# Three shared buffers for parts and fifth product, a tile of group 0 in another PSUM bank, and one relu part placed earlier

## The chip, the cores and the metric

The program runs on one core of one Trainium2 chip. The metric is the time of one execution on the device, in microseconds (us). The kernel before the change was run three times: 630.22, 631.93 and 632.46 us, median 631.93. The profiled execution, from which all rows here are read, took 632.26 us itself; its span from the first to the last instruction is 630.5 us, so 1.76 us lie around the span.

## The reference, cut to what matters

Three layers follow each other on 1152 tokens of width 512: windowed attention (8 heads), a soft mixture of four experts, and a dense layer with a rational activation.

```python
attn = softmax(where(mask, scale * q @ k.T, -1e9)) @ v        # 2 x 8 heads x 576 x 64
x = attn.transpose(0, 2, 1, 3).reshape(1152, 512)
p = domain_probs / (domain_probs.sum(-1, keepdims=True) + 1e-9)
x = sum(p[:, e:e+1] * (relu(x @ w1[e]) @ w2[e]) for e in range(4))   # hidden width 1024
h = x @ w_in                                                   # 2048 wide; w_in, w_out in float64
g = (a0 + a1*h + a2*h**2 + a3*h**3) / (1 + |b0|*|h| + |b1|*h**2 + 1e-6)
out = g @ w_out
```

## The kernel before, in words

Tokens lie in three chunks `c` of 384 (nine token tiles `t` of 128, three in each chunk). The hidden widths of both matrix layers are cut into units `u` of 256 columns. Units 0 to 15 belong to the experts, units 16 to 23 to the dense layer; two units make a group `g` (groups 0 to 7 experts, 8 to 11 dense). For a unit and a chunk a *first product* (`h_bank`, line 467) makes the hidden values in PSUM (tile `ps_h`), and for a group and a token tile a *second product* (`o_half`, line 513, once for each of the group's two units) makes 128 x 512 outputs in PSUM (tile `ps_o`). Operands are kept as a high part and a low part, so a product is three passes: high by high, high by low, low by high. In most units two of the three chunks are made together in seven smaller products instead (`product`, lines 943 and 1246); the fifth of them is copied to SBUF (`p5`) and added to other products in PSUM by VectorE (lines 969 and 1263).

PSUM has eight banks: two for `ps_o`, four for the two-bank tiles `ps_h` of the pool `psh`, two for a third `ps_h` tile (pool `psh3`, used by every third `h_tile()` that is not told otherwise). During attention the last two hold `ps_s`.

What sets the order of work:

- *Attention* follows the table `ATTENTION`.
- *The experts* (`for g in range(NG1)`) are written in the order of TensorE. Work for VectorE and ScalarE is put between by a planner: `Pace.pe` is TensorE's planned time, `Pace.dv` VectorE's. `later(wait, cost, key, f)` gives a step a due time of `Pace.pe + wait`; when TensorE's planned time passes it, the step is written. Gaps are filled (`fill`) with prepared steps (weight splits at lines 829 and 833, token sums) and with the conversion of the dense weights from float64 words (`convert`, lines 241 to 311), which is needed only by the dense part. So one changed wait shifts VectorE's planned time, and with it the order of all later filling on VectorE, ScalarE and SP. `settle(key)` writes a pending step at once when TensorE needs it.
- *The dense part* follows the table `DENSE`. In it `o9.6.0` is the second product of group 9, token tile 6, first unit; `z9.6` moves that tile out of PSUM; `P5.22` is the fifth product of unit 22, `F22` its copy to SBUF, `v22` and `q22` the two adds that read it. For groups 9 and 10 `z` is a copy by ScalarE into a buffer `part` (line 1162) and a DMA by GpSimd's queue that adds the buffer to `acc[t]` in SBUF (line 1163). There are 18 such tiles and 6 fifth products. The next use of a buffer waits until its DMA has landed, or, for `p5`, until `q` has read it.

The pools that the change touches: `part` had two buffers and `p5` one of its own in pool `late` (lines 1161 and 1259).

Of the kernel before, what the change touches and what calls it, by code (L numbers as in the profile page):

```python
# [18 lines left out]
F32 = mybir.dt.float32  # L19
# [10 lines left out]
NT, DM = 1152, 512  # L30
# [4 lines left out]
TC = 384  # L35
# [60 lines left out]
COST = dict(h=2.09, p=1.045, o=2.74, osum=0.78, relu=1.0, add=0.59, split=0.68, sums=0.42, bits=0.41, both=1.15, token=1.0)  # L96
# [5 lines left out]
def body(ctx, tc, qkv, mask, dp, w1, w2, w1d, w2d, coef, out):  # L102
# [15 lines left out]
    def h_tile(last=None):  # L118

        count[0] += 1  # L120
        last = third and count[0] % 3 == 0 if last is None else last
        pool = third[0] if last else psh
        return pool.tile([128, 2, 512], F32, tag="h", name="ps_h")
# [337 lines left out]
    def h_bank(u, c, i, ps, ks=range(4)):  # L461
        wh, wl = weight(w1s, u, 4)
        xh, xl = xt[c]
        for k in ks:
            f = slice(i * 128, (i + 1) * 128)
            for n, (a, b) in enumerate(((wh, xh), (wh, xl), (wl, xh))):
                nc.tensor.matmul(  # L467
                    ps[:, i, :TC], lhsT=a[:, k, f], rhs=b[:, k],
                    start=k + n == 0, stop=k + n == 5,
                )  # L470
# [46 lines left out]
    def o_bank():  # L517
        return pso.tile([128, 512], F32, tag="o", name="ps_o")
# [11 lines left out]
    def by_dma(g, t):  # L530
        return (1, 3) <= (g, t) < (NG1 - 1, 0)
# [28 lines left out]
    class Rational:  # L560
# [53 lines left out]
        def high(self):  # L614
            self.hh, self.hl = new_h(self.u, self.c)
            nc.scalar.copy(self.hh, self.u1)
# [6 lines left out]
    with tc.manual_schedule():  # L623
# [83 lines left out]
        def small_loads():  # L707
# [5 lines left out]
            v=lambda r: units[r].load_values(),  # L713
# [3 lines left out]
            g=small_loads,  # L717
# [78 lines left out]
        def later(wait, cost, key, f):  # L796
            Pace.due.append((Pace.pe + wait, cost, key, f))
# [102 lines left out]
        def h_begin(u, c, last=None):  # L900
            settle(("w1", u))
            begun[u, c] = h_tile(last)
            h_bank(u, c, 0, begun[u, c])
            passed(COST["h"])

        def h_paced(u, c, last=None):
            if (u, c) not in begun:
                h_begin(u, c, last)
            ps = begun[u, c]
            h_bank(u, c, 1, ps)  # L910
            passed(COST["h"])
            high, low = relu_parts(u, c, ps)
            high()
            later(1.1, COST["relu"], ("h", u, c), low)

        def o_paced(g, t, wait=0.0):
            for v in range(2):
                settle(("h", 2 * g + v, t // 3))
                settle(("w2", 2 * g + v))
            ps = o_bank()  # L920
            for v in range(2):
                o_half(g, t, v, ps)
            passed(COST["o"])
            if by_dma(g, t):
                if wait:
                    later(wait, 0.0, ("o", g, t), lambda: o_sum(g, t, ps))
                else:
                    o_sum(g, t, ps)
            else:
                later(0.2, COST["osum"], ("o", g, t), lambda: o_sum(g, t, ps))  # L930
# [100 lines left out]
        for g in range(NG1):  # L1031
            u = 2 * g
            again = g + 1 in BLOCKED
            o = lambda *at: [(o_paced, *i) for i in at]
            if g == 0:
                later(0.0, COST["osum"], ("o", 0, 3), lambda: o_sum(0, 3, ps_2[3]))
                token_sums()
                tokens_later(temp[0], *(t[:, 0] for t in tt))
                sums_later(2)
                sums_split_later(2, 1)  # L1040
                o_paced(0, 4)
                o_paced(0, 5)
                for v in range(2):
                    h_paced(v, 2)
                tokens_later(temp[2], *(t[:, :2] for t in xt[2]), "first")
                sums_split_later(2, 0)
                tokens_later(temp[1], *(t[:, 1] for t in tt), "second")
                sums_later(3)
                tokens_later(temp[3], *(t[:, 2] for t in tt), "third", begin_conversion)
                continue  # L1050
            a, b = (Blocks(v) for v in (u, u + 1))
            w2_loads = (load_w2, u + 2), (load_w2, u + 3)
            free = [(load_w1, u + 3)] * (g > 1) + [w2_loads[0]] * (g == 1) + [w2_loads[1]]
            free = [(weights_free, *free)] if again else []
            run = lambda g, *ts: [o_paced(g, t, 1.5 * (n == 2)) for n, t in enumerate(ts)]

            def next_sums():
                if again:
                    sums_later(u + 2)
                    sums_split_later(u + 2, 1)  # L1060
                    split_later(w2s, "w2", u + 2)
                    split_later(w1s, "w1", u + 3)
                else:
                    loads((load_w1, u + 3))

            if g == 1:
                sums_split_later(u + 1, 1)
                split_later(w1s, "w1", u + 2)
                a.first(False)
                o_paced(0, 6)  # L1070
                a.sixth()
                a.fifth()
                a.sum_up(0.8, False)
                o_paced(0, 7)
                a.seventh()
                a.second()
                sums_split_later(u + 1, 0, free)
                o_paced(0, 8)
            else:
                for v in (u, u + 1):  # L1080
                    new_h(v, 0)
                h_paced(u, 0, False)
                sums_split_later(u + 1, 1)
                split_later(w2s, "w2", u + 1)
                if again:
                    split_later(w1s, "w1", u + 2)
                run(g - 1, 6, 7, 8)
                a.first(False)
                h_paced(u + 1, 0, True)
                a.fifth()  # L1090
                a.sixth()
                a.sum_up(0.2, False)
                run(g - 1, 3, 4)
                sums_split_later(u + 1, 0, free)
                o_paced(g - 1, 5, 1.5)
                a.seventh()
                a.second()
            b.first(True)
            a.third()
            a.fourth()  # L1100
            next_sums()
            b.fifth()
            b.sixth()
            b.sum_up(0.2, False)
            run(g, *range(3 if again else 1))
            b.seventh()
            b.second()
            if again:
                h_begin(u + 2, 0, False)
            else:  # L1110
                o_paced(g, 1)
            b.third()
            b.fourth()
            if g == 1:
                Window.spare[:] = [None, lone[:, 0], lone[:, 1]]
            if again:
                sums_split_later(u + 2, 0, [(loads, (load_w1, u + 4))])
                sums_later(u + 3)
            else:
                loads(*w2_loads, (load_w1, u + 4), (load_w1, u + 5))  # L1120
# [11 lines left out]
        early_open, late = tc.tile_pool(name="early", bufs=1), []  # L1132
# [3 lines left out]
        ps_h, ps_2, p5_ps, p5s, x2_ps, turned, copied, rational = {}, {}, {}, {}, {}, set(), {}, {}  # L1136
# [18 lines left out]
        def sum_up(g, t, cols=0):  # L1155
            ps, s = ps_2.pop((g, t, cols)), columns(cols)
            if g == NG1:
                acc[t] = accp.tile([128, DM], F32, tag=f"acc{t}", name=f"acc{t}")
                nc.scalar.copy(acc[t], ps)
            elif NG1 < g < NG - 1:  # L1160
                part = late[0].tile([128, DM], F32, tag="part", name="part", bufs=2)
                nc.scalar.copy(part, ps)  # L1162
                nc.gpsimd.dma_start(acc[t], part, accum_op=ALU.add)  # L1163
            elif cols:
                nc.vector.tensor_tensor(out=acc[t][:, s], in0=ps, in1=acc[t][:, s], op=ALU.add)
                store(t, s)
            else:
                o_sum(g, t, ps)
# [86 lines left out]
        def fifth(u):  # L1255
            if not late:
                early_open.__exit__(None, None, None)
                late.append(ctx.enter_context(tc.tile_pool(name="late", bufs=1)))
            p5s[u] = late[0].tile([128, TC], F32, tag="p5", name="p5")
            nc.scalar.copy(p5s[u], p5_ps[u])  # L1260

        def add_fifth(i, u):
# [4 lines left out]
        def of(name):  # L1267
# [3 lines left out]
            h=bank, o=second, O=lambda *a: second(*a, of="h"), z=sum_up, x=turn, X=x_high, Y=x_low, W=x_whole,  # L1271
            T=token_sum, C=sum_high, S=sum_low, P=product, Z=seed, F=fifth,
            v=lambda u: add_fifth(0, u), q=lambda u: add_fifth(1, u),
# [116 lines left out]
```

## Time and profile before

| | |
|---|---|
| median of three runs | 631.93 us |
| profiled execution | 632.26 us, span 630.5 us |
| TensorE matmul busy | 621.4 us, 99% of the span |
| VectorE busy | 522.0 us, 83% |
| ScalarE busy | 371.9 us, 59% |
| GpSimd busy | 88.4 us, 14% |
| mean granted TensorE clock | 0.997 |

The table is read by its first busy row: TensorE works nearly the whole span, so a change of the time has to come from its few idle stretches, from its clock, or from new idle stretches. The experts' part runs from about 80 to 410 us, the dense part from there to the end. In stretches of 5 to 20 us the granted clock is 1.00 everywhere but from 560 to 570 us and at the very end.

### The profile page before, as it was taken

How to read it: one execution, taken by the hardware profiler on the slowest of the kernel's cores; microseconds unless marked ns; L12 is line 12 of the kernel's file. 1: busy time of each engine (PE TensorE's matmuls, PEld its weight loads, DVE VectorE, ACT ScalarE, POOL GpSimd, SP SyncE). 2: the span in 40 equal slices, each digit the busy share in tenths (PEclk: the TensorE clock that was granted, in tenths of full speed). 3: DMA queues.
4: the chain of work that ended last, by engine and by line, in shares of the span. 5: the costliest groups of instructions: out<-in, count | busy, mean ns of one | idle time of the engine just before them, and what ended most of it. 6: DMA issues, size and time to landing. Idle time of an engine off the chain costs nothing.

```text
span 630.5 us, 9862 instructions
## 1 busy us (share of the span) xinstructions
PE 621.4 (99%) x3728; PEld 556.0 (88%) x3728; DVE 522.0 (83%) x788; ACT 371.9 (59%) x682; POOL 88.4 (14%) x103
## 2 busy tenths in 40 slices
PE   8999999999999999999999999999999999989997
PEld 4888898999999999999999999898989989969886
DVE  7687488798888888888888898839999998979894
ACT  6787625364555555555555555346786887768660
POOL 2223330011111111111111111000000011120110
PEclk9999999999999999999999999999999999989999
DMA  9944302368789679788778789762221484471233
GB/s 295 318 141 166 115 8 68 100 181 247 209 227 247 208 218 249 214 221 237 220 223 234 227 263 247 252 269 105 97 100 43 150 275 101 105 206 25 50 84 116
DMA packets 39535, 111.28 MB, mean 177 GB/s; under 512 B 4256, under 2 KB 5024, under 8 KB 37440
## 3 DMA queue, kind: packets, MB, share of 16 engines
q1 hardware_dynamic: 29104, 92.14, 43.4%
q0 software_dynamic: 9936, 18.09, 16.4%
q8 instruction: 29, 0.48, 0.3%
q10 hardware_dynamic: 448, 0.43, 0.3%
q14 instruction: 18, 0.15, 0.1%
HBM read 67.13 MB, written 25.43 MB: 147 GB/s over the span
## 4 chain that ended last, share of the span: by engine, by line
PE 70%; issue 25%; DMA 1%; DVE 1%; POOL 1%; ACT 0%; POOLq 0%; ACTq 0%
PE ps_o L513 33%; PE ps_h L467 14%; PE ps_h L943 12%; PE ps_o L943 2%; PE ps_h L1246 2%; PE ps_v L431 2%; DMA acc<-part 1%; PE ps_s L417 1%; PE ps_h L513 1%; POOL acc L1163 1%; PE ps_s L362 1%; PE ps_h L655 1%; PE ps_o L1246 0%; DVE mx L390 0%; DVE pr L380 0%
## 5 line engine op out<-in xcount | busy, mean ns | idle before, releaser
L513 PE MATMUL ps_o<-w,hh 128*128 128x512 f32 x848 | 229.1, 392 | 2.8 <-ACT part L1162 2.6
L513 PEld LDWEIGHTS ps_o<-w,hh 128*128 128x128 f32 x848 | 157.8, 188 | 34.3 <-ACT part L1162 3.0
L513 PE MATMUL ps_o<-w,hl 128*128 128x512 f32 x424 | 131.1, 391 | 0.1
L467 PE MATMUL ps_h<-xh,w 128*128 128x384 f32 x464 | 126.0, 338 | 0.0
L513 PEld LDWEIGHTS ps_o<-w,hl 128*128 128x128 f32 x424 | 79.6, 188 | 17.5 <-DVE hl L489 0.6
L467 PEld LDWEIGHTS ps_h<-xh,w 128*128 128x128 f32 x464 | 84.4, 188 | 1.2 <-issue 0.3
L544 POOL DMA_DIRECT2D acc<-part x51 | 45.3, 889 | 258.0 <-ACT part L543 201.1
L467 PE MATMUL ps_h<-xl,w 128*128 128x384 f32 x232 | 77.6, 334 | 0.0
L543 ACT ACTIVATE part<-ps_o,p_sb 128x512 f32<-128x512 f32 x51 | 35.1, 688 | 48.8 <-issue 22.7
L485 ACT ACTIVATE hh<-ps_h 128x768 fp32r<-128x768 f32 x48 | 39.0, 812 | 42.1 <-PE ps_h L943 31.6
L489 DVE SCALAR_TENSOR_TENSOR hl<-ps_h,hh 128x768 fp32r<-128x768 f32 x48 | 45.0, 951 | 4.0 <-ACT hh L485 3.7
L1163 POOL DMA_DIRECT2D acc<-part x18 | 15.6, 868 | 204.1 <-ACT part L1162 197.9
L467 PEld LDWEIGHTS ps_h<-xl,w 128*128 128x128 f32 x232 | 43.6, 188 | 0.1
L969 DVE TENSOR_TENSOR ps_h<-ps_h,p 128x384 f32<-128x384 f32 x28 | 15.8, 566 | 23.3 <-PE ps_h L943 23.3
L271 ACT ACTIVATE x<-x 128x512 f32<-128x512 f32 x32 | 21.7, 677 | 22.7 <-DVE t L268 20.5
L943 PE MATMUL ps_h<-t,sw 128*128 128x384 f32 x168 | 34.0, 337 | 0.0
L396 ACT ACTIVATE pr<-pr,mx 128x80 f32<-128x80 f32 (+1 forms) x84 | 29.7, 358 | 6.0 <-DVE mx L390 4.7
L833 DVE TENSOR_TENSOR w<-raw,w 128x512 fp32r<-128x512 f32 x48 | 32.8, 684 | 0.5 <-ACT w L829 0.5
L943 PEld LDWEIGHTS ps_h<-t,sw 128*128 128x128 f32 x168 | 29.9, 188 | 1.2
L943 PE MATMUL ps_h<-xh,w 128*128 128x384 f32 x104 | 29.7, 335 | 0.0
L573 ACT ACTIVATE ab<-ps_h,absb 128x768 f32<-128x768 f32 x24 | 21.8, 907 | 13.3 <-DMA w<-w 7.9
L592 DVE TENSOR_TENSOR u<-ps_h,u 128x768 f32<-128x768 f32 x24 | 22.9, 953 | 7.6 <-ACT u L577 6.1
(162 smaller groups left out, 1145.8 us busy)
## 6 DMA issues: line engine op xcount, KB each, us to landing
acc<-part POOLq DMA_DIRECT2D x69, 256.0 KB, 5.5
raw<-in_w_dram SPq DMA_DIRECT2D x32, 512.0 KB, 6.4
w<-w SPq DMA_DIRECT2D x14, 1024.0 KB, 6.3
w<-lone SPq DMA_DIRECT2D x18, 512.0 KB, 4.6
x<-in_w1d_dram SPq DMA_DIRECT2D x16, 512.0 KB, 4.5
x<-in_w2d_dram SPq DMA_DIRECT2D x16, 512.0 KB, 5.5
w<-w SPq DMA_DIRECT2D x14, 512.0 KB, 5.9
sw<-sw SPq DMA_DIRECT2D x12, 512.0 KB, 5.8
```

Source lines behind the costliest of these rows:

```text
L396: nc.scalar.activation(pr[:, j, i], pr[:, j, i], AF.Exp, scale=-1.0, bias=self.mx[:, j, i:i + 1], accum_out=self.total[:, j, i:i + 1],)
L467: nc.tensor.matmul(ps[:, i, :TC], lhsT=a[:, k, f], rhs=b[:, k], start=k + n == 0, stop=k + n == 5,)
L485: nc.scalar.activation(hh, ps[:, :, :TC], AF.Relu)
L489: nc.vector.scalar_tensor_tensor(out=hl, in0=ps[:, :, :TC], scalar=0.0, in1=hh.bitcast(F32), op0=ALU.max, op1=ALU.subtract,)
L513: nc.tensor.matmul(ps, lhsT=a[:, i, tk], rhs=b[:, i, cols], start=v + n == 0, stop=v + n == 6)
L543: nc.scalar.activation(part, ps, AF.Copy, scale=pe)
L544: nc.gpsimd.dma_start(acc[t], part, accum_op=ALU.add)
L573: nc.scalar.activation(self.ab, self.ps, AF.Abs, scale=absb[:, 0:1])
L592: nc.vector.tensor_tensor(out=self.u1, in0=self.ps, in1=self.u1, op=ALU.mult)
L833: nc.vector.tensor_tensor(out=w[:, 1, s_], in0=raws[nm, u][:, s_], in1=w[:, 0, s_].bitcast(F32), op=ALU.subtract)
L943: nc.tensor.matmul(out, lhsT=a[i][:, k], rhs=b[j][:, k], start=first and k + n == 0, stop=k + n == 3, skip_group_check=not first,)
L1163: nc.gpsimd.dma_start(acc[t], part, accum_op=ALU.add)
```

## The change

Three edits.

1. The buffers of `part` in the dense part become three, and `p5` is taken from the same three (`tag="part"`, the first 384 of 512 columns) instead of having one buffer of its own. A buffer is handed out in the order in which buffers come free.
2. The tile of `o_paced(0, 4)` (group 0, token tile 4) is put into the first bank of an `h_tile()` instead of an `o_bank()`. This `h_tile()` is the one that falls on the third pool; the tiles of units 0 and 1, chunk 2, come one place later in the rotation and both lie in `psh`.
3. For unit 1, chunk 2, the low part of relu (line 489, `hl`) is due 0.1 us after its planned time instead of 1.1.

```diff
-        def h_paced(u, c, last=None):
+        def h_paced(u, c, last=None, wait=1.1):
...
-            later(1.1, COST["relu"], ("h", u, c), low)
+            later(wait, COST["relu"], ("h", u, c), low)
-        def o_paced(g, t, wait=0.0):
+        def o_paced(g, t, wait=0.0, ps=None):
...
-            ps = o_bank()
+            ps = ps if ps is not None else o_bank()
...
-                o_paced(0, 4)
+                o_paced(0, 4, ps=h_tile()[:, 0])
                 o_paced(0, 5)
                 for v in range(2):
-                    h_paced(v, 2)
+                    h_paced(v, 2, wait=1.1 - v)
...
-                part = late[0].tile([128, DM], F32, tag="part", name="part", bufs=2)
+                part = late[0].tile([128, DM], F32, tag="part", name="part", bufs=3)
...
-            p5s[u] = late[0].tile([128, TC], F32, tag="p5", name="p5")
+            p5s[u] = late[0].tile([128, DM], F32, tag="part", name="p5", bufs=3)[:, :TC]
```

TensorE's order is the same before and after but for the name of the bank of `o_paced(0, 4)`. GpSimd's is the same too. ScalarE's order in the dense part is the same; what changes there is what the copies wait for. The first place is ScalarE from `z9.8` to `z10.1`; `DMASW` with a digit is the semaphore of an adding DMA (they go round eight, so that `z9.6` to `z10.1` signal 1, 2, 3, 4, 5), `PE_49`, `DVE_49` and `Activation_49` are those of the engines. Before:

```order
L1162 COPY part<-ps_o 128x512 [waits DMASW1_49,PE_49,Activation_49]
L586 ACTIVATE ab<-sq,cbias 128x768 [waits DVE_49,Activation_49]
L577 ACTIVATE u_5549<-ps_h,na 128x768 [waits Activation_49]
L573 ACTIVATE ab<-ps_h,absb 128x768
L589 ACTIVATE ab<-ab 128x768 [waits Activation_49]
L1162 COPY part<-ps_o 128x512 [waits DMASW2_49,PE_49]
L586 ACTIVATE ab<-sq,cbias 128x768 [waits DVE_49]
L577 ACTIVATE u_5574<-ps_h,na 128x768 [waits DVE_49]
L1162 COPY part<-ps_o 128x512 [waits DMASW3_49,PE_49]
```

After the change, the same nine:

```order
L1162 COPY part<-ps_o 128x512 [waits PE_49]
L586 ACTIVATE ab<-sq,cbias 128x768 [waits DVE_49,Activation_49]
L577 ACTIVATE u_5549<-ps_h,na 128x768 [waits Activation_49]
L573 ACTIVATE ab<-ps_h,absb 128x768
L589 ACTIVATE ab<-ab 128x768 [waits Activation_49]
L1162 COPY part<-ps_o 128x512 [waits DMASW1_49,PE_49]
L586 ACTIVATE ab<-sq,cbias 128x768 [waits DVE_49]
L577 ACTIVATE u_5574<-ps_h,na 128x768 [waits DVE_49]
L1162 COPY part<-ps_o 128x512 [waits DMASW2_49,PE_49]
```

Nothing moved; `z9.8` waits for no DMA any more, `z10.0` for the one of `z9.6` instead of `z9.7`, `z10.1` for the one of `z9.7` instead of `z9.8`.

The second place is VectorE at the two relu parts of chunk 2 in group 0 (`hl_1278` of unit 0, `hl_1311` of unit 1; `xl2` the low part of a token sum; `sw` the low part of summed weights). Before:

```order
L489 SCALAR_TENSOR_TENSOR hl_1278<-ps_h_1242,hh_1277 128x768
L862 TENSOR_TENSOR sw_1294<-raw_767,sw_1294 128x512
L893 TENSOR_TENSOR xl2_122<-ab_1203,xh2_121 128x768
L489 SCALAR_TENSOR_TENSOR hl_1311<-ps_h_1280,hh_1310 128x768
L862 TENSOR_TENSOR sw_1322<-raw_767,sw_1322 128x512
```

After:

```order
L489 SCALAR_TENSOR_TENSOR hl_1278<-ps_h_1242,hh_1277 128x768
L862 TENSOR_TENSOR sw_1294<-raw_767,sw_1294 128x512
L489 SCALAR_TENSOR_TENSOR hl_1311<-ps_h_1280,hh_1310 128x768
L893 TENSOR_TENSOR xl2_122<-ab_1203,xh2_121 128x768
L862 TENSOR_TENSOR sw_1337<-raw_767,sw_1337 128x512
```

Unit 1's relu part went ahead of `xl2`.

The third place is VectorE just ahead of the tenth add of a fifth product (line 969), as one of many places where the filling of the experts' part shifted. Before:

```order
L311 SCALAR_TENSOR_TENSOR sums<-x_2194,sums 128x512
L258 TENSOR_SCALAR t<-x_2270 128x512
L862 TENSOR_TENSOR sw<-raw,sw 128x512
L268 SCALAR_TENSOR_TENSOR t<-x_2270,t 128x512
L969 TENSOR_TENSOR ps_h<-ps_h,p_2227 128x384
```

After:

```order
L311 SCALAR_TENSOR_TENSOR sums<-x_2172,sums 128x512
L258 TENSOR_SCALAR t<-x_2254 128x512
L268 SCALAR_TENSOR_TENSOR t<-x_2254,t 128x512
L245 TENSOR_TENSOR w<-sums,w 128x512
L862 TENSOR_TENSOR sw<-raw,sw 128x512
L167 TENSOR_TENSOR sums<-sums 128x2x128 x3
L969 TENSOR_TENSOR ps_h<-ps_h,p_2228 128x384
```

More of the conversion (lines 245 and 167) now stands ahead of this add.

## Rows read from the trace of the kernel before

**Rows 1.** The page's first part: busy time, share, instructions of each engine.

```profile
PE 621.4 (99%) x3728; PEld 556.0 (88%) x3728; DVE 522.0 (83%) x788; ACT 371.9 (59%) x682; POOL 88.4 (14%) x103
```

**Rows 2.** Waits of TensorE: engine, line waited for, total us, times, longest.

```profile
PE ps_o L513 <- ACT part L1162: 2.6, 1, 2.6
...
PE ps_o L513 <- DVE xl L455: 0.3, 1, 0.3
```

**Rows 3.** Stretches: length, busy PE, PEld, DVE, ACT, POOL, granted clock, DMA share, GB/s.

```profile
560.00:565.00 5.00, 2.50 (x6) 2.02 (x7) 1.72 (x2) 2.89 (x4) 0.88 (x1) 0.74 0.82 214
565.00:570.00 5.00, 5.00 (x27) 4.90 (x27) 4.96 (x7) 2.52 (x4) 0.87 (x1) 0.92 0.44 76
```

**Rows 4.** Timeline of TensorE, 553 to 575: start, length, instruction, idle before.

```profile
558.41 1.07 PE L513 MATMUL ps_o<-w,hh 128*128 128x512 f32 x4
559.32 0.61 PE L513 MATMUL ps_o<-w,hl 128*128 128x512 f32 x2
562.50 2.07 PE L513 MATMUL ps_o<-w,hh 128*128 128x512 f32 x4 [2.56 <-ACT part L1162]
...
570.71 0.33 PE L1246 MATMUL ps_o<-xh,sw 128*128 128x384 f32 x1
```

**Rows 5.** Timeline of ScalarE around the same wait.

```profile
557.66 0.88 ACT L589 ACTIVATE ab<-ab 128x768 f32<-128x768 f32 x1
561.86 0.59 ACT L1162 COPY part<-ps_o 128x512 f32<-128x512 f32 x1 [3.32 <-DMA acc<-part]
...
563.18 0.98 ACT L577 ACTIVATE u<-ps_h,na 128x768 f32<-128x768 f32 x1
564.22 0.59 ACT L1162 COPY part<-ps_o 128x512 f32<-128x512 f32 x1
```

**Rows 6.** Line 1163, the adding DMA: two single ones, then all eighteen.

```profile
L1163 POOL DMA_DIRECT2D acc<-part x1: 872/872/872, 548.2 to 548.2; - x1
DMA to landing us min/median/max: 5.8/5.8/5.8
...
L1163 POOL DMA_DIRECT2D acc<-part x1: 859/859/859, 552.8 to 552.8; - x1
DMA to landing us min/median/max: 9.0/9.0/9.0
...
DMA to landing us min/median/max: 3.2/3.3/9.1
```

**Rows 7.** Timeline of TensorE, 74 to 102: group 0's second products.

```profile
77.04 0.61 PE L513 MATMUL ps_o<-w,hl 128*128 128x512 f32 x2
77.93 1.19 PE L513 MATMUL ps_o<-w,hh 128*128 128x512 f32 x4 [0.28 <-DVE xl L455]
...
94.30 1.08 PE L513 MATMUL ps_o<-w,hh 128*128 128x512 f32 x4
95.51 0.73 PE L513 MATMUL ps_o<-w,hl 128*128 128x512 f32 x2
96.08 1.21 PE L943 MATMUL ps_h<-t,sw 128*128 128x384 f32 x6
```

**Rows 8.** Timeline of ScalarE, 74 to 104: relu of unit 1, chunk 2.

```profile
92.06 0.81 ACT L485 ACTIVATE hh<-ps_h 128x768 fp32r<-128x768 f32 x1 [1.87 <-PE ps_h L467]
```

**Rows 9.** Timeline of VectorE at five places of the argument.

```profile
93.63 0.96 DVE L893 TENSOR_TENSOR xl<-ab,xh 128x768 fp32r<-128x768 f32 x1 [2.33 <-ACT xh L890]
94.50 0.95 DVE L489 SCALAR_TENSOR_TENSOR hl<-ps_h,hh 128x768 fp32r<-128x768 f32 x1
...
201.13 0.57 DVE L969 TENSOR_TENSOR ps_h<-ps_h,p 128x384 f32<-128x384 f32 x1 [1.45 <-PE ps_h L943]
...
564.19 0.96 DVE L592 TENSOR_TENSOR u<-ps_h,u 128x768 f32<-128x768 f32 x1 [3.28 <-ACT u L577]
...
573.06 0.57 DVE L1263 TENSOR_TENSOR ps_h<-ps_h,p 128x384 f32<-128x384 f32 x1 [1.34 <-PE ps_h L1246]
```

**Rows 10.** Timeline of TensorE: the product that the add at 201.13 precedes.

```profile
201.97 0.33 PE L943 MATMUL ps_h<-xh,sw 128*128 128x384 f32 x1
```

## The prediction, made before the changed kernel ran

> **What bounds the kernel now.** I read the busy shares first: TensorE is busy for 621.4 us of a 630.5 us span [rows 1], so no other engine can give time except through TensorE's idle stretches and its clock. The list of TensorE's waits comes next [rows 2]. It has one large entry, 2.6 us in a single wait for ScalarE's copy of `part`, and one small entry of 0.3 us for line 455, a VectorE step of attention. The experts' part has no entry of its own between 100 and 410 us: there TensorE is never late, and nothing can be won, only lost. The table of stretches then shows that the large wait costs twice: the granted clock is 0.74 from 560 to 565 us and 0.92 from 565 to 570 [rows 3], and 1.00 before and after. In the timeline four passes that take 0.91 us from start to start at 558.41 are followed, at 562.50, by four that last 2.07 [rows 4].
>
> The large wait, read backwards. TensorE at 562.50 begins `o10.2`. There are two `ps_o` banks, so it needs the bank of `o10.0`, which ScalarE's copy `z10.0` empties from 561.86 on. ScalarE itself had stood idle for 3.32 us, and what ended that is a landing DMA [rows 5]. With two `part` buffers `z10.0` uses the buffer of `z9.7`, two copies back, whose DMA was issued at 552.8 and took 9.0 us, so it landed at 561.8 [rows 6]. The other adding DMAs took 3.3 us in the median.
>
> **The change part by part.** All durations are of the profiled execution (632.26 us itself, 0.33 above the median of the runs shown, 631.93).
>
> *Three buffers.* By the semaphores in the order, `z10.0` now waits for the DMA of `z9.6`: issued at 548.2, landed 5.8 us later, at 554.0 [rows 6]. That is over by the time `o10.0` is complete. In the row before it ScalarE ends `e21.1` at 557.66 + 0.88 = 558.54 [rows 5]; the tile is complete by then, since TensorE was in the next tile's last half from 558.41 on [rows 4]. So `z10.0` runs from about 558.5 to 559.1 instead of 561.86 to 562.45. TensorE has run out of other work at 559.32 + 0.45 = 559.77 (two passes at half of the 0.91 that four take), 0.6 us later than the bank is empty, and goes straight on. Gain: 562.50 - 559.77 = 2.73 us of waiting. The clock does not fall, which gives back 5 x 0.26 + 5 x 0.08 = 1.70 us [rows 3]. Together 4.43 us.
>
> What is late next? `z10.1` is two places behind on ScalarE. It now waits for the DMA of `z9.7`, landing at 561.8, and ScalarE reaches it at about 560.8 (after `z10.0`, an L586 and the L577 that stood at 563.18), so ScalarE stands for about 1 us with this copy at its head; behind it in the queue are L569 and the high part `H21.1`. Who needs that? TensorE needs the bank of `z10.1` for the fifth product at 570.71, which moves to 570.71 - 4.43 = 566.28. The copy is over at 561.8 + 0.6 = 562.4, so 3.9 us remain. The ScalarE step at 563.18 feeds VectorE's step at 564.19, which had waited 3.28 us for it [rows 9]. It comes at about 559.8, a gain of 3.4 us where TensorE gains 4.4. The missing 1.0 us is covered by the 1.34 us that VectorE stands idle at 573.06 waiting for TensorE [rows 9]; after that both run to TensorE's pace again, with the same distances as before. Later copies wait for DMAs at least two copies older, or for an add on VectorE that stands ahead in program order; `F22` and `F23`, which had their own buffer, now wait for the DMAs of `z9.8` and `z10.1`. `z9.8` stands ahead of the step at 557.66 on ScalarE, so its DMA is issued by then; even at the longest landing, 9.1 us [rows 6], it is there by 566.8, while the fifth product of unit 22, which `F22` reads, only begins at 566.28. I count these at nothing.
>
> A rule that would undo all this: the Trainium skill, page "DMA: Bandwidth & Descriptors", section on the anatomy of one DMA on GpSimd's path, fits 2.0 us plus the bytes at 436 GB/s. For 256 KB that is an estimate of 2.6 us. By it the DMA issued at 552.8 would land at 555.4, no buffer would be missing, and the sum below would hold only the 0.86 us of the experts' part. The row says 9.0 us for this one, and ScalarE's wait ends as it lands; the row decides.
>
> *Another bank for tile 4 of group 0.* Before, `o_paced(0, 4)` waits for a `ps_o` bank that line 455 reads last. From the pair of passes at 77.04 to the next start at 77.93 are 0.89 us; two passes take 0.45; the wait costs 0.44 us [rows 7]. In its new bank the tile waits for TensorE's own earlier work only. The next tile needs the `ps_o` bank of line 455 1.4 us later and has it. The rotation of `ps_h` moves by one: the first product of the seven in group 1 now needs the bank that unit 0's relu part read. That part is done before VectorE's idle stretch that ends at 93.63, so by 93.63 - 2.33 = 91.30 at the latest [rows 9]; TensorE gets there at about 91.4, so nothing is added. Gain 0.44.
>
> *Unit 1's relu part.* TensorE needs it for the passes at 95.51. The four passes at 94.30 take 1.21 us to the next start instead of 0.91, and the two behind 0.57 instead of 0.45: 0.42 us [rows 7]. The relu part starts at 94.50, after `xl2`, which itself waited until 93.63 for ScalarE [rows 9]; its own input was ready at 92.06 + 0.81 = 92.87 [rows 8]. In front of `xl2` it ends at about 93.8, more than 1 us before its use even with TensorE 0.44 us earlier. `xl2` then starts at about 93.7, 0.1 us later than before. Gain 0.42.
>
> *What the planner does with it.* Summed over both orders at the durations of the rows, up to 8.7 us of VectorE work, the conversion, comes ahead of adds and relu parts that TensorE waits for, against before. Bounds: nothing, if VectorE's idle time takes it; 8.7 us less 0.3 of slack if none does. I went through all 26 later adds of line 969 and compared, at the durations of their rows, what stands between an add and the add or relu part before it. The worst rise is 0.6 us. At the add at 201.13 it is 0.5 us (one L245 and three L167 come in, an L289 and an L298 go out), and VectorE stood idle for 1.45 us there [rows 9]. The add has 0.28 us of slack to the product at 201.97 [rows 10], and this too stays, since the idle time takes the rise. I take nothing, nearest to these rows.
>
> Sum: 4.43 + 0.44 + 0.42 = 5.29 us. Against its own execution 632.26 - 5.29 = 626.97; a median lies 0.33 lower by the runs shown, so 626.7 us.
>
> **The rivals.**
>
> *The wait moves on.* Three adding DMAs are now in flight while weights are loaded, and `z10.0`'s leaves at about 559.4 instead of 562.85. If the shared traffic makes all of them land 9.1 us after the last, at 568.5, `z10.1` ends at 569.1, the fifth product waits 2.8 us, the clock falls again (1.7), and 4.5 of the 5.3 us are gone: 631.2. A smaller slip gives 627 to 631. For it: 9.0 us happened here with two buffers. Against it: the landing would have to slip from 561.8 to past 565.7. The Trainium skill, page "DMA: Bandwidth & Descriptors", section "Issuing engines are not separate DMA queues", says that DMAs of all issuing engines run on the same 16 engines and interleave; by that rule the earlier issue slows those already under way. No run here shows yet by how much. Chance 0.12.
>
> *VectorE is late instead.* If the idle 1.34 us at 573.06 does not cover the missing 1.0, TensorE waits 1.0 us, and if the clock falls with it, 1.7 more: 627.7 to 629.4. Against it: the idle row itself. Chance 0.07.
>
> *Slower, by the planner.* VectorE's idle time in the experts' part is in truth latency of the conversion (its steps wait for ScalarE), and does not take the extra work. Then the adds come late by up to 8.7 - 0.3 = 8.4 us in all: 631.9 + 8.4 - 5.3 = 635.0, and 636.7 if the clock falls once. It decides as soon as more than 5.3 of the 8.7 us are not absorbed. For it: 0.28 us of slack. Against it: the idle rows name TensorE, not ScalarE, as what ended them. Chance 0.06.
>
> *It doesn't do what it says.* `z10.0` waits for something else as long (a pass of ScalarE, another landing): only 0.86 us remain, 631.1. Against it: the semaphores in the order. Chance 0.05.
>
> **How the numbers follow.** The forecast, 626.7, has a chance of 0.70 (its own range 625.9 to 627.6). About 0.5%, 3.2 us, is what a measurement of this kernel can tell from no change, so "faster" ends at 628.8. To it go the forecast, nearly all of "VectorE is late" (0.06) and under half of "the wait moves on" (0.05): 0.81. "Same" gets the rest of these, the case without effect, and a little of the planner's: 0.14. "Slower" is 0.05. For eight in ten the range runs from 625.8, a little under the forecast's own end, to 629.6, which takes in "VectorE is late" and the smaller slips.
>
> **What would show it.** Right: no TensorE wait for line 1162 in the list, the granted clock 1.00 from 500 to 620 us; no wait for line 455 near 78 us; the passes of tile 6 of group 0 in even steps of 0.91 and 0.45; VectorE idle before each second add still over 0.3 us; the end of the dense part 5 us earlier. Wrong: a TensorE wait for ScalarE at a fifth product (first rival), for VectorE after 570 us (second), or for line 969 between 100 and 400 us (third); or `z10.0` still behind a DMA (fourth).

## The result and the profile after

The kernel after the change takes 626.31 us in the median of six runs (625.88 to 627.53); the kernel before, in six runs, 631.86 us (630.22 to 633.04). The ratio is 0.992, with a 95% interval of 0.9907 to 0.9934: faster by 0.66% to 0.93%, which is over the 0.5% that the prediction called the least that can be told from no change. The forecast was 626.7 us, in a range of 625.8 to 629.6.

The profiled execution of the new kernel took 627.53 us itself, the highest of the six, with a span of 625.7 us. The page's first part answers to [rows 1]: TensorE has 2.5 us less busy time, the other engines nearly the same. The program has as many matmuls as before (3728 weight loads in both; the records of two matmuls are missing here). The busy time falls because passes at the lower clock last longer: the four at 562.50 took 2.07 us, and the same four take 1.07 us now, at 559.35 below.

```profile
PE 618.9 (99%) x3726; PEld 555.1 (89%) x3728; DVE 522.2 (83%) x788; ACT 370.9 (59%) x682; POOL 88.0 (14%) x103
```

TensorE's waits after the change (engine, line waited for, total us, times, longest) are the whole answer of that view:

```profile
PE ps_h L655 <- DVE warm L645: 1.2, 1, 1.2
PE ps_s L362 <- DMA qk<-in_qkv_dram: 0.9, 1, 0.9
PE ps_h L362 <- DMA qk<-in_qkv_dram: 0.6, 1, 0.6
PE ps_s L417 <- POOL pr L406: 0.2, 1, 0.2
PE ps_h L655 <- issue: 0.2, 1, 0.2
```

Both entries of [rows 2] are gone, and what is left stands in the attention part, before 76 us, which the change doesn't touch. (There the kernel before had two waits of 1.2 us, for lines 645 and 406, that [rows 2] leaves out and that the prediction's account of the list doesn't count.) The two stretches of [rows 3], by the same columns, read after:

```profile
560.00:565.00 5.00, 5.00 (x29) 4.86 (x28) 4.96 (x6) 3.19 (x5) 0.87 (x1) 1.00 1.05 246
565.00:570.00 5.00, 5.00 (x29) 4.74 (x28) 4.59 (x7) 4.39 (x7) 0.00 (x0) 1.00 0.10 16
```

TensorE is busy for all of both, and its granted clock is 1.00 (2.4 GHz) where it was 0.74 and 0.92. The timeline of TensorE answers to [rows 4]: `o10.2`, at 559.35, follows the passes of 558.89 after 0.46 us, the time of two passes, with no wait.

```profile
558.89 0.61 PE L513 MATMUL ps_o<-w,hl 128*128 128x512 f32 x2
559.35 1.07 PE L513 MATMUL ps_o<-w,hh 128*128 128x512 f32 x4
...
565.93 0.33 PE L1246 MATMUL ps_o<-xh,sw 128*128 128x384 f32 x1
```

The timeline of ScalarE in the same stretch answers to [rows 5]: `z10.0` at 557.97 waits for nothing, and the wait for a landing DMA has moved to `z10.1`, behind two further steps, where it is 1.28 us long.

```profile
557.97 0.62 ACT L1162 COPY part<-ps_o 128x512 f32<-128x512 f32 x1
...
559.28 1.03 ACT L577 ACTIVATE u<-ps_h,na 128x768 f32<-128x768 f32 x1
561.59 0.59 ACT L1162 COPY part<-ps_o 128x512 f32<-128x512 f32 x1 [1.28 <-DMA acc<-part]
```

The adding DMAs, answering to [rows 6]: those issued at 552.4 and 555.3, then all eighteen.

```profile
L1163 POOL DMA_DIRECT2D acc<-part x1: 859/859/859, 552.4 to 552.4; - x1
...
DMA to landing us min/median/max: 9.1/9.1/9.1
...
L1163 POOL DMA_DIRECT2D acc<-part x1: 862/862/862, 555.3 to 555.3; - x1
...
DMA to landing us min/median/max: 8.1/8.1/8.1
...
DMA to landing us min/median/max: 3.2/3.3/9.1
```

The DMAs have not become quicker: the long landing is still 9.1 us. What changed is that nobody on TensorE's path stands behind it. In group 0, TensorE's timeline answers to [rows 7]: from 77.74 to 78.19 are 0.45 us instead of 0.89, and the tile now lies in a `ps_h` bank; from 94.41 the steps are 0.92 and 0.45 us instead of 1.21 and 0.57.

```profile
77.74 0.62 PE L513 MATMUL ps_o<-w,hl 128*128 128x512 f32 x2
78.19 1.07 PE L513 MATMUL ps_h<-w,hh 128*128 128x512 f32 x4
...
94.41 1.08 PE L513 MATMUL ps_o<-w,hh 128*128 128x512 f32 x4
95.33 0.62 PE L513 MATMUL ps_o<-w,hl 128*128 128x512 f32 x2
95.78 1.23 PE L943 MATMUL ps_h<-t,sw 128*128 128x384 f32 x6
```

VectorE's timeline, three places of [rows 9]: the relu part now starts at 93.02, ahead of `xl2`; the step that had waited 3.28 us for ScalarE waits for nothing (560.40); and the idle time ahead of the add of `v22` has shrunk from 1.34 to 0.37 us.

```profile
93.02 0.96 DVE L489 SCALAR_TENSOR_TENSOR hl<-ps_h,hh 128x768 fp32r<-128x768 f32 x1 [1.03 <-ACT hh L485]
...
560.40 0.95 DVE L592 TENSOR_TENSOR u<-ps_h,u 128x768 f32<-128x768 f32 x1
...
568.28 0.57 DVE L1263 TENSOR_TENSOR ps_h<-ps_h,p 128x384 f32<-128x384 f32 x1 [0.37 <-PE ps_h L1246]
```

Last, the 28 adds of fifth products in the experts' part: VectorE stood idle before 17 of them until TensorE's product came, and the list of who waited for them is empty.

```profile
L969 DVE TENSOR_TENSOR ps_h<-ps_h,p x28: 554/567/567, 98.6 to 401.2; 128x384 f32<-128x384 f32 x28
...
  PE ps_h L943: 16.7, 17
...
who waited for it (us, times):
```

To compare profiled executions without the attention part, whose length differs from one to the next (TensorE's first pass of line 513 behind the last attention step starts between 75.63 and 76.73 us in the eleven executions), I use the time from that pass to the start of the last passes of line 513. Before: 76.03 to 626.57, 550.54 us. After: 76.73 to 621.76, 545.03 us. By this measure the change is worth 5.51 us; the other kernels are given against 550.54 too. About 0.2 us of such a difference is not the edits': the twelve passes of line 1178 near 437 us take 1.68 us in the first execution of the kernel before and 1.47 in a second one, of the same program, and in the kernel after:

```profile
437.67 1.68 PE L1178 MATMUL ps_h<-ident,acc 128*128 128x128 f32 x12
...
437.90 1.47 PE L1178 MATMUL ps_h<-ident,acc 128*128 128x128 f32 x12
```

### The profile page after: what moved, and what is told of

It reads as the page before. It is cut to its first block, busy times and chain, and to the rows that moved or that the text cites. A ratio compares the mean times of both kernels' runs of the same rounds, so it can differ in the third digit from the quotient of the medians.

```text
span 625.7 us, 9862 instructions
## 1 busy us (share of the span) xinstructions
PE 618.9 (99%) x3726; PEld 555.1 (89%) x3728; DVE 522.2 (83%) x788; ACT 370.9 (59%) x682; POOL 88.0 (14%) x103
## 4 chain that ended last, share of the span: by engine, by line
PE 98%; DMA 1%; DVE 0%; issue 0%
PE ps_o L513 46%; PE ps_h L467 22%; PE ps_h L943 14%; PE ps_h L1246 6%; PE ps_o L943 2%; PE ps_v L431 2%; PE ps_h L513 2%; PE ps_s L417 1%; DMA qk<-in_qkv_dram 1%; PE ps_o L1246 1%; PE ps_s L362 1%; PE ps_h L655 1%; PE ps_h L1178 1%; PE ps L362 0%; PE ps_h L362 0%; DVE acc L552 0%
## 5 line engine op out<-in xcount | busy, mean ns | idle before, releaser
L513 PE MATMUL ps_o<-w,hh 128*128 128x512 f32 x840 | 225.8, 390 | 0.0
L513 PEld LDWEIGHTS ps_o<-w,hh 128*128 128x128 f32 x840 | 155.9, 188 | 30.3
L513 PE MATMUL ps_o<-w,hl 128*128 128x512 f32 x420 | 129.4, 389 | 0.0
L857 ACT CAST sw<-raw 128x512 fp32r<-128x512 f32 x28 | 17.2, 615 | 21.2 <-DVE raw L167 19.0
```

What stands on the lines that cost most here:

```text
L513: nc.tensor.matmul(ps, lhsT=a[:, i, tk], rhs=b[:, i, cols], start=v + n == 0, stop=v + n == 6)
```

## The experiments

Theory A was the prediction's: a copy behind a long landing holds TensorE and its clock; edits 2 and 3 each give back one small wait; the planner's reorder costs nothing. The rivals were that the gain of edit 1 needs the other edits, that something other than the missing buffer holds `z10.0`, and that the reorder costs time. Edit 1 alone, edits 2 and 3 alone, the later loads and the other work for TensorE shared 23 runs of the kernel before, median 632.23 us (630.17 to 633.77).

**Edit 1 alone.**

```diff
-                part = late[0].tile([128, DM], F32, tag="part", name="part", bufs=2)
+                part = late[0].tile([128, DM], F32, tag="part", name="part", bufs=3)
-            p5s[u] = late[0].tile([128, TC], F32, tag="p5", name="p5")
+            p5s[u] = late[0].tile([128, DM], F32, tag="part", name="p5", bufs=3)[:, :TC]
```

> Edit 1 alone on the kernel before (three buffers shared by part and fifth product). My theory: it carries the dense part's gain, 2.73 us of waiting and 1.70 us of clock, and nothing else; 632.26 - 4.43 on its own execution, so about 627.5 us median. TensorE has no wait for line 1162, the granted clock is 1.00 from 560 to 570 us, and the waits near 78 us (0.28) and 95 us (passes 1.21 instead of 0.91 apart) are still there. Rival: the other two edits, by the new order of the conversion, helped the dense part too; then this one alone stays at 628.5 or above.

It took 627.62 us (627.06 to 628.32, six runs), ratio 0.9927 (0.9911 to 0.9942); by the trace 546.19 us, 4.35 less. In TensorE's waits there is no line 1162, and the small wait of [rows 2] stands as before:

```profile
PE ps_o L513 <- DVE xl L455: 0.3, 1, 0.3
```

So edit 1 brings its 4.4 us without the others. A third buffer beside a `p5` of its own was not run, so what the sharing with `p5` does by itself is not shown.

**Edits 2 and 3 alone.**

```diff
-                o_paced(0, 4)
+                o_paced(0, 4, ps=h_tile()[:, 0])
...
-                    h_paced(v, 2)
+                    h_paced(v, 2, wait=1.1 - v)
```

> Edits 2 and 3 without edit 1. My theory: 0.44 + 0.42 us less, about 631.0 us; no wait near 78 and 95 us; no TensorE wait between 100 and 410 us though VectorE's order is another; the wait for line 1162 is still 2.5 to 2.8 us and the granted clock from 560 to 565 still about 0.74. Rival (planner): VectorE's new order costs, 632 us or above with waits for line 969. Rival (conversion done earlier helps the start of the dense part): under 630 us.

631.16 us (629.29 to 632.55, twelve runs), ratio 0.9987 (0.9974 to 1.0): with that interval the times taken together do not show it. Runs with the same mean granted clock do: the eleven at 0.997 have a median of 631.21 us, and the seventeen at 0.997 of the kernel before 632.36, 1.15 us more. In the trace TensorE has no wait for line 455 and none for line 969, so here the reorder, which comes from edit 3 alone, costs it nothing. One thing in it was unexpected. TensorE waited again for `z10.0`, and yet its clock stayed at 1.00:

```profile
560.99 1.20 PE L513 MATMUL ps_o<-w,hh 128*128 128x512 f32 x4 [2.47 <-ACT part L1162]
```

```profile
560.00:565.00 5.00, 4.01 (x21) 3.75 (x22) 2.28 (x3) 3.67 (x5) 1.75 (x2) 1.00 0.67 143
565.00:570.00 5.00, 5.00 (x30) 4.98 (x29) 4.97 (x6) 4.40 (x7) 0.00 (x0) 1.00 0.30 52
```

Its trace gives 547.75 us, 2.79 less than before. Of this 1.70 are the clock that did not fall, and 1.09 are left: 0.99 where the two edits act (0.55 at 78 us and 0.44 at 94), and the rest is in line 1178 and the length of the wait, which differ between executions.

**Each of these two by itself, run once.**

```diff
-                o_paced(0, 4)
+                o_paced(0, 4, ps=h_tile()[:, 0])
```

> Edit 2 alone (tile 4 of group 0 in the third pool's bank). VectorE's order does not change but for that tile's name. TensorE has no wait for line 455 near 78 us: 0.44 us less there, 631.5; the passes of tile 6 near 95 us still 1.21 us apart; the wait for line 1162 unchanged. If the shifted rotation of the first products' banks costs anything, a TensorE wait for line 489 shows at the first product of group 1 near 91.5 us.

The passes of 77.28 are followed at 77.74, 0.46 us later, so the gain there comes from the bank: 0.44 us in the wait and 0.11 more, as the next four passes take 0.90 us to the following start (77.74 to 78.64) where they took 1.03 behind the wait. The step of 94 us is as before (93.95 to 95.17, 1.22 us). By the trace 550.10 us, 0.44 less; that this is the forecast's figure is chance, since the bank's 0.55 and 0.18 in line 1178 are met by a longer wait for line 1162 in this execution (2.9 us). Timeline of TensorE:

```profile
77.28 0.62 PE L513 MATMUL ps_o<-w,hl 128*128 128x512 f32 x2
77.74 1.07 PE L513 MATMUL ps_h<-w,hh 128*128 128x512 f32 x4
```

```diff
-                    h_paced(v, 2)
+                    h_paced(v, 2, wait=1.1 - v)
```

> Edit 3 alone (unit 1's relu low part 1 us earlier by plan). VectorE's order changes in the whole experts' part. TensorE: passes near 95 us 0.91 and 0.45 apart, 0.42 us less there, 631.5; wait near 78 us unchanged at 0.28; no wait between 100 and 410 us; the wait for line 1162 unchanged. Rival: a wait for line 969, 489 or 833 somewhere in the experts' part.

Here the step of 94 us is even (0.92 and 0.45 us) and the wait for line 455 is there (0.27 us at 78.21). But by the trace the kernel is only 0.19 us shorter, at 550.35. All of the gain is given back at one add of the experts' part: TensorE stands idle for 0.32 us (the last of these rows) and, with the slower passes around the gap, falls back by about 0.6 us against the kernel before.

```profile
94.56 1.08 PE L513 MATMUL ps_o<-w,hh 128*128 128x512 f32 x4
95.48 0.62 PE L513 MATMUL ps_o<-w,hl 128*128 128x512 f32 x2
...
361.56 0.44 PE L943 MATMUL ps_h<-xh,sw 128*128 128x384 f32 x1 [0.32 <-DVE ps_h L969]
```

VectorE's rows give the cause. The conversion step of line 258 ahead of this add waits 2.98 us for its load, which SP issued at 352.8 us; for the step at this place in the kernel before, at 355.8 us, the last such load had been issued at 340.9 and there was no wait. The add behind it starts at 360.95 where it started at 359.32 (last row, before), after idle time that TensorE's product ended:

```profile
358.80 0.43 DVE L258 TENSOR_SCALAR t<-x 128x512 uint32<-128x512 uint32 x1 [2.98 <-DMA x<-in_w2d_dram]
...
360.95 0.56 DVE L969 TENSOR_TENSOR ps_h<-ps_h,p 128x384 f32<-128x384 f32 x1
...
359.32 0.57 DVE L969 TENSOR_TENSOR ps_h<-ps_h,p 128x384 f32<-128x384 f32 x1 [1.87 <-PE ps_h L943]
```

In the experts' part VectorE, ScalarE and GpSimd have the same order here as with edits 2 and 3 together and as in the whole change. In the other four executions of that order the same step waits 0.30 to 1.52 us for its load, and TensorE does not wait. So it is the wait for the load that differs; whether the missing bank has a part in it, one execution cannot show. The single times, 632.06 and 632.4 us, decide nothing.

**The other DMAs away instead of a third buffer.** The kernel before, two buffers, with the loads of the second matrix of units 22 and 23 (`j22`, `j23`) issued behind `z10.1`, by ScalarE:

```diff
-k23.1 ... o9.8.0 j22 L20.1 z9.7
-u21.1 d21.1 o9.8.1 j23 H20.2 ...
-... n22.0 z10.1 h23.0.0 s22.0 r21.1
+k23.1 ... o9.8.0 L20.1 z9.7
+u21.1 d21.1 o9.8.1 H20.2 ...
+... n22.0 z10.1 j22 j23 h23.0.0 s22.0 r21.1
```

> The kernel before with its two part buffers, but the two last weight loads (second weights of units 22 and 23, 1 MB each as the profile counts them), which SP issued at 553.2 and 554.5 us, are issued by ScalarE right behind z10.1. Nothing else changes. My theory: the 9.0 us landing of the adding DMA issued at 552.8 is the traffic of these loads; without them it lands in 3 to 4 us, by 557, z10.0 waits for no DMA, TensorE does not stall, the clock stays at 1.00: the same 4.4 us as three buffers give, about 627.5 us. Rival: the landing is long by itself (three adding DMAs close together, or the add), it still takes 7 us or more, and the time stays at 631.9.

627.52 us (627.04 to 628.2, six runs), ratio 0.9929 (0.9914 to 0.9943), the same as edit 1 alone. The DMA that `z10.0` waits for now lands in a third of the time:

```profile
L1163 POOL DMA_DIRECT2D acc<-part x1: 859/859/859, 553.0 to 553.0; - x1
...
DMA to landing us min/median/max: 3.3/3.3/3.3
```

So the 9.0 us of [rows 6] come from the weight loads beside it, and are no property of the adding DMA. The Trainium skill, page "DMA: Bandwidth & Descriptors", section "Issuing engines are not separate DMA queues", says that DMAs started by the scalar, sync or gpsimd engine run on the same 16 DMA engines and interleave; this trace agrees, with 3.3 against 9.0 us for one transfer. The loads did not vanish: the two adding DMAs issued beside them, at 559.6 and 561.8, now take 7.1 and 8.9 us, but no copy waits for either. ScalarE's one wait for a landing in this kernel, 2.68 us at 604.92, stood in the kernel before too (2.76 us at 609.13), and no TensorE wait follows it:

```profile
604.92 0.59 ACT L1162 COPY part<-ps_o 128x512 f32<-128x512 f32 x1 [2.68 <-DMA acc<-part]
...
609.13 0.59 ACT L1162 COPY part<-ps_o 128x512 f32<-128x512 f32 x1 [2.76 <-DMA acc<-part]
```

**The change and the later loads together.** The same edit of `DENSE` and of the loads' engine, on the kernel after the change.

> The changed kernel, with the two last weight loads issued by ScalarE behind z10.1 as in e4. My theory: what is left of the long landing is ScalarE's 1.3 us in front of z10.1, and this is off TensorE's path: the wait goes, the time stays at 626.3 (within 0.3). Rival: ScalarE's 1.3 us still cost TensorE something later in the dense part; then 625.3 or less.

626.66 us (625.94 to 628.06, six runs), ratio 0.9913 (0.9892 to 0.9933) to 632.6 us of the kernel before on that chip; by the trace 545.05 us, where the change alone has 545.03. The two cures are for one wait, and the second adds nothing.

**Other work for TensorE in the wait.** The kernel before, two buffers, with `h23.0` ahead of the first half of `o10.2`:

```diff
-... u22.0 o10.2.0 t21.1 n22.0 z10.1 h23.0.0 s22.0 r21.1
-f21.1 h23.0.1 N22.0 ...
+... u22.0 h23.0.0 t21.1 n22.0 z10.1 h23.0.1 s22.0 r21.1
+f21.1 o10.2.0 N22.0 ...
```

> The kernel before with two part buffers, but TensorE does the first product of unit 23, chunk 0 (24 passes, 4.1 us, in a free bank) ahead of o10.2.0, so it has work while z10.0 waits for its DMA. VectorE's and ScalarE's orders are unchanged. Theory A: the wait also holds ScalarE's queue, and behind it VectorE; that chain is not earlier than before, so the stall moves to the next bank that VectorE empties (first product P1.23, about 574 us): a TensorE wait for VectorE of about 2.4 us, and if the clock falls with it about 1.7 more; 630.0 to 631.8 us. Theory B: only the ps_o bank mattered; TensorE then gains 4.2 us, about 627.7, with no wait behind it.

631.18 us (630.14 to 632.18, twelve runs), ratio 0.9985 (0.9974 to 0.9996). TensorE goes on at 559.59 and runs for 7.9 us, but `z10.0` still waits 3.40 us with all of ScalarE's queue behind it, and the delay reaches TensorE at 569.49: the sixth product of unit 22 needs a seed in PSUM that ScalarE copies at 568.96 (line 1253). I had expected a wait of about 2.4 us for VectorE at the first product of unit 23, near 574 us: the size was near, engine and place were wrong. TensorE's timeline, then ScalarE's:

```profile
559.59 0.41 PE L467 MATMUL ps_h<-xh,lone 128*128 128x384 f32 x1
...
569.49 1.32 PE L1246 MATMUL ps_h<-t,sw 128*128 128x384 f32 x6 [2.03 <-ACT ps_h L1253]
```

```profile
561.45 0.58 ACT L1162 COPY part<-ps_o 128x512 f32<-128x512 f32 x1 [3.40 <-DMA acc<-part]
...
568.96 0.48 ACT L1253 COPY ps_h<-ps_h 128x384 f32<-128x384 f32 x1
```

Its trace is 1.73 us shorter than before (548.81), no more than the 1.70 us of a clock that did not fall in this execution. The runs say the same: the eight with a mean clock of 0.999 or 1.00 have a median of 630.85 us, where such runs of the kernel before have 630.63; the small ratio comes from more of the runs keeping their clock. The wait itself was only moved. What has to be freed is ScalarE's queue, which edit 1 does.

**Does the clock fall each time?** The kernel before, and the one with edits 2 and 3 alone, once more each.

> The kernel before, without any edit, once more: is the fall of TensorE's clock behind the wait for line 1162 a fixed consequence of that wait, or does it come in some executions and not in others? Theory A (it differs between executions, since the wait of 2.5 us in the run with edits 2 and 3 alone left the clock at 1.00 where 2.56 us in the kernel before were followed by 0.74): the wait is 2.3 to 2.9 us again, and the clock from 560 to 570 us is either below 0.95 for some 3.4 us, with a span near 630.5, or 1.00, with a span near 629. Theory B (edits 2 and 3 do something to the clock): the clock falls again, as in the first profile, by 1.7 us.

> Edits 2 and 3 alone once more, the same program as the one whose clock stayed at 1.00. Theory A: the wait for line 1162 is 2.3 to 2.9 us again and the clock may fall this time; with a fall the span is near 629.5 to 630, without one near 627.5. Theory B: the clock stays at 1.00 and the span near 627.5 again.

The kernel before waited 2.74 us and its clock fell; its span is 630.8 us:

```profile
560.00:565.00 5.00, 2.26 (x7) 1.77 (x7) 1.54 (x3) 2.78 (x4) 0.88 (x1) 0.80 0.77 212
565.00:570.00 5.00, 5.00 (x27) 4.90 (x26) 4.96 (x7) 2.39 (x3) 0.87 (x1) 0.86 0.50 86
```

The lost share is 5 x 0.20 + 5 x 0.14 = 1.70 us, as in [rows 3]; by the measure of the trace this second execution has 550.62 us, where the first had 550.54. The other waited 2.69 us, and its clock did not fall:

```profile
560.00:565.00 5.00, 3.15 (x16) 2.88 (x17) 1.58 (x3) 3.23 (x5) 1.48 (x2) 1.00 0.77 177
565.00:570.00 5.00, 5.00 (x31) 5.00 (x30) 4.96 (x6) 3.90 (x6) 0.27 (x1) 1.00 0.31 53
```

The mean granted clock of each timed run decides between the theories A (the fall comes in some executions only) and B (edits 2 and 3 do something to the clock) of these two expectations. Of the 23 runs of the kernel before, 17 have a mean of 0.997, with a median of 632.36 us, and 6 a mean of 1.00, with 630.63 us: 1.73 us apart. On the chip of the single edits it is 8 of 11 at 0.995 to 0.997, with 632.85 us, and 3 at 1.00, with 630.70. On the chip of these last two, one more run of the kernel before had 1.00, with a span of 629.3 us where its profiled execution had 630.8. And 11 of the 12 runs of edits 2 and 3 had 0.997, so these edits do nothing to the clock. Theory A holds: the same program, with the same wait, loses 1.7 us of clock in some executions and not in others. The wait is what it hangs on: in the 24 timed runs of the four kernels in which TensorE does not wait there (the change, edit 1 alone, the later loads, and both together) no mean clock is under 0.999.

## Why the prediction was right, point by point

- *Three buffers.* Right: 4.43 us were forecast, 4.35 by the trace of edit 1 alone. `z10.0` waits for no DMA, `z10.1` waits about 1 us (1.28), and its copy ends at 562.18, 3.75 us before the fifth product at 565.93; 3.9 were forecast. One path the forecast did not name: the sixth product needs the seed that ScalarE copies (line 1253), the place where the delay came out when TensorE was given other work. ScalarE's idle time ahead of line 573, the step before that copy, went from 1.18 us (first row, before) to 0.20 us (second row, after). It held, but the prediction had not worked that out:

```profile
569.87 0.91 ACT L573 ACTIVATE ab<-ps_h,absb 128x768 f32<-128x768 f32 x1 [1.18 <-PE ps_h L467]
...
565.09 0.91 ACT L573 ACTIVATE ab<-ps_h,absb 128x768 f32<-128x768 f32 x1 [0.20 <-PE ps_h L467]
```

- *VectorE's cover.* Right: the idle time before the add of `v22` was to shrink by 1.0 us and shrank by 0.97 (1.34 to 0.37). 0.37 us of that cover are left.
- *The clock's 1.70 us.* Right for the profiled execution from which the sum was made, wrong as a fixed term. Against the runs of the kernel before at clock 1.00 the change is worth 630.63 - 626.31 = 4.32 us, and against those at 0.997 it is 632.36 - 626.31 = 6.05; both are estimates, since the kernel after ran in another series. The clocks of the runs beside it are not on record, but their median (631.86 us) lies nearer to the second sort. So the forecast of the median met it partly by luck: in a series with more runs at 1.00 the change would have been worth up to 1.7 us less.
- *The bank and the relu part.* Right in place, and nearly in size: 0.44 and 0.42 us were forecast, 0.55 and 0.44 are read at 78 and 94 us, with each edit alone and with both. The 0.11 us more at 78 us are the slower passes right behind the wait, which the forecast left out.
- *The planner's reorder at nothing.* Right for the whole change, but the reason was incomplete. The prediction bounded the added VectorE work before an add, 0.6 us at the worst, and took VectorE's idle time to cover it. It did not count that a conversion step can stand waiting for its own load. With the relu part alone that made one add come 1.6 us later and cost TensorE more than the edit's whole gain; in the whole change the same step waited 0.30 us, and that this was short enough is luck as far as the prediction goes.
- *The sum.* 5.29 us were forecast (which is 626.64 by its own figures), 5.51 by the trace, 5.55 between the medians. By the trace the wait and clock are worth 4.35, the bank 0.55, the relu part 0.44; the 0.2 left over are the passes of line 1178 named above, and not the change's.
- *The rivals.* The wait did not move on to a fifth product: the DMA issued at 552.4 landed 9.1 us later, at 561.5 (before: 9.0, at 561.8), and the one issued at 559.0 in 5.7. VectorE was not late, the planner cost TensorE nothing in this execution, and the edit did what it says.

## What to carry to other kernels

A copy that waits for a buffer holds its whole engine, and what is queued behind it pays as well; ask for a buffer whose DMA is long over, rather than for other work to put in the gap. One more buffer, paid for by letting two small uses share a set, cures the same wait as moving the transfers that slow the DMA; one cure is enough. And when a wait ends in a fallen clock, look at the mean clock of every run before a sum is made against one profile: the median of a few runs can fall on either side. When filling work is moved ahead of an add, count the loads that it waits for, and not only its duration.

## What was not expected of the hardware

- After a wait of 2.3 to 2.9 us the granted clock fell to 1.2 GHz, the lower of its two levels (a cost of 1.70 us each time), in four profiled executions (the kernel before, twice, and each of edits 2 and 3 by itself), and it stayed at 2.4 GHz in two, after 2.47 and 2.69 us (edits 2 and 3 together). So the length of the wait alone does not decide it. What does stays open.
- An adding DMA of one size (256 KB) takes 3.3 us, or up to 9.1 us when weights are being loaded beside it.
